# One-token attention and gated unit: every large load split by even and odd partitions over two DMA queues

## The chip, the cores and the metric

The kernel runs on one core of a Trainium2 chip. The core has a matrix engine (TensorE, PE in the profile), a vector engine (VectorE, DVE), a scalar engine (ScalarE, ACT), a general engine (GpSimd, POOL), an engine for synchronisation (SyncE, SP), and 16 DMA engines that move data between the chip's memory (DRAM in the names) and the core's own memory of 128 partitions. SyncE, ScalarE and GpSimd can issue transfers; each has its own queue. The metric is the time of one execution in microseconds (us), as the median of several. The profile's span, from the first to the last instruction, is a little shorter.

## The reference

Two branches work on one token `x` of 512 numbers, and a scalar gate mixes them. Everything is bfloat16.

```python
g = sigmoid((x * gate_w).sum())
# A: attention over the last W = 4096 positions of a cache of 65536
q = x @ wq                                  # 32 heads of 128; wq is 512 x 4096
s = q . k_cache[:, last 4096] * 128**-0.5   # 8 key heads, each used by 4 query heads
o = softmax(s) . v_cache[:, last 4096]
a = o @ wo                                  # wo is 4096 x 512
# B: gated unit
b = (sigmoid(x @ w_gate) * (x @ w_up)) @ w_down     # 512 -> 1792 -> 512
out = g * a + (1 - g) * b
```

With one token every weight and every cached key and value is used once. Read are 4 MB of wq, 8 MB of keys, 8 MB of values, 4 MB of wo and three matrices of 1.75 MB, 30.67 MB in the profile's count. The result is 512 numbers.

## The kernel before

All large loads are issued by SyncE, in the order in which they are needed, each as one transfer over all 128 partitions. `a` counts pairs of key heads; partition p = 2x + y of a tile of keys or values holds 64 consecutive positions of head 2a + y.

```python
nc.scalar.dma_start(xr[:, 0, :], A_x[0, :, :])               # x and gate_w: 1 KB each, by ScalarE
nc.scalar.dma_start(xr[:, 1, :], gate_w...)
dq = nc.sync
dq.dma_start(wq_sb[:], wq_v)                                 # 128 rows of 32 KB

def load_pair(t, cache, a, n0=0, n1=NP):
    dq.dma_start(t[:, n0:n1, :]..., cache[0, 2*a:2*a+2, SBASE:SBASE+W, :]...)    # 128 rows of 16 KB

kn = [...]                       # 4 tiles of keys, buffers "blk" (4 of them)
for a in range(HP): load_pair(kn[a], A_k_cache, a)
dq.dma_start(wg_sb[:], ...)      # w_gate
dq.dma_start(wu_sb[...], ...)    # w_up without its last part
for h in range(2):
    for b in range(2):           # the last part of w_up: 4 loads of 32 partitions
        dq.dma_start(wx_sb[32*b:32*b+32, h, :], wx_v[h, b])
vv = [...]                       # 4 tiles of values, in the buffers of the keys
for a in range(HP): load_pair(vv[a], A_v_cache, a)
for c0 in (0, 16): dq.dma_start(wo_sb[:, c0:c0+16, :], ...)          # wo in two halves
for j0, j1 in ((0,8), (8,11), (11,13), (13,14)):
    dq.dma_start(wd_sb[:, j0:j1, :], ...)                            # w_down in four parts

make_identity(nc, identf[:])     # GpSimd: identity and constants
...
for _ in range(4): nc.vector.memset(spare[:], 0.0)
...
```

After the front (x turned, the gate) the work follows the loads:

```python
# q = x @ wq, copied and transposed                       (needs wq)
# keys: VectorE transposes each tile (kT), TensorE multiplies into S_ps     (needs kn)
# gate branch, maximum, exponential, eT = transposed weights
for a in range(HP):
    for m in range(NP // 4):
        nc.tensor.matmul(pv_ps[32*a:32*a+32], lhsT=eT[:, a, 4*m:4*m+4, :], rhs=vv[a][:, 4*m:4*m+4, :], ...)
# up branch (glu), then o_ps -> oT -> oX -> oY: one column of oY for each 128 rows of wo
for c in range(NC_O): add_row(oY[:, c:c+1], wo_sb[:, c, :], ...)     # 32 x 2 matmuls
for j in range(NJ):   add_row(hT[:, j, 0:1], wd_sb[:, j, :], ...)    # 14 x 2 matmuls
nc.vector.tensor_copy(res[:, 0:HN], ...); nc.scalar.copy(res[:, HN:], ...)
nc.scalar.dma_start(out[0, :, :], res[:])
```

## Time and profile before

| | |
|---|---|
| time, median of 3 | 80.55 us (80.54 to 81.8) |
| span of the profiled execution | 78.7 us |
| TensorE busy | 52.5 us (67%) |
| VectorE busy | 38.8 us (49%) |
| ScalarE / GpSimd busy | 10.9 / 3.3 us |
| DMA | 30.71 MB in 2616 packets, mean 390 GB/s |
| tile of keys: issue to landing | 27.2 us (median of 4) |
| tile of values: issue to landing | 19.1 us (median of 4) |

How to read it: PE, DVE, ACT and POOL rows cut the span into 40 slices of about 2 us; each digit is the busy share in tenths. The DMA row is the mean busy share of the 16 DMA engines. "q1" is a DMA queue; its row gives packets, MB, and the time of its packets as a share of 16 engines' span. A line such as L290 is a line of the kernel. "out<-in" names the tile that an instruction writes and those that it reads. "<-DMA x" after an idle time says that a transfer into x ended the wait. The chain that ended last follows the last instruction back to what released it, step by step.

### The profile page before, as it was taken

To read this page: it belongs to the slowest core of one execution; us is meant where nothing else is said; L and a number is where in the kernel's file an instruction comes from. 1 tells how busy PE (TensorE), PEld (TensorE's weight loads), DVE (VectorE), ACT (ScalarE), POOL (GpSimd) and SP (SyncE) were. 2 spreads that over 40 slices of the span, in tenths; PEclk is the share of its full clock that TensorE was granted. 3 is DMA by queue.
4 is the path that set the end of the run, shared out by engine and by line. 5 is a ranking of instruction groups with operands and counts; after the bars stand their busy time and mean duration, and the time that the engine had idled before them with its cause. 6 is when DMAs were issued, how large, how long until landed. Compare 5 with 4: busy or idle time off the path is not lost.

```text
span 78.7 us, 798 instructions
## 1 busy us (share of the span) xinstructions
PE 52.5 (67%) x314; PEld 23.6 (30%) x314; DVE 38.8 (49%) x52; ACT 10.9 (14%) x20; POOL 3.3 (4%) x10
## 2 busy tenths in 40 slices
PE   0200094999905788898887307999996799567650
PEld 0200041344302333333332202344341345345420
DVE  1600920029869999999986349962000000690020
ACT  2400000247651000000002191000000002000010
POOL 7900000000000000000000000000000000000000
PEclk9999999999999999999999995699999999999997
DMA  7779799999999999999999999999999999999710
GB/s 184 300 316 533 316 483 391 408 425 458 441 408 416 425 474 416 386 437 417 438 410 426 441 416 441 408 433 441 416 433 433 424 425 433 416 391 409 290 42 1
DMA packets 2616, 30.71 MB, mean 390 GB/s; under 512 B 307, under 2 KB 438, under 8 KB 822
## 3 DMA queue, kind: packets, MB, share of 16 engines
q1 hardware_dynamic: 2608, 30.67, 92.9%
q8 instruction: 2, 0.03, 0.2%
q10 hardware_dynamic: 6, 0.00, 0.0%
HBM read 30.67 MB, written 0.00 MB: 390 GB/s over the span
## 4 chain that ended last, share of the span: by engine, by line
DMA 93%; SPq 2%; PE 1%; DVE 1%; issue 0%
DMA wd_sb<-in_B_w_down_dram 36%; DMA kn<-in_A_k_cache_dram 32%; DMA vv<-in_A_v_cache_dram 24%; SPq L84 2%; PE a_ps L290 1%; DVE res L341 1%; SPq L80 0%
## 5 line engine op out<-in xcount | busy, mean ns | idle before, releaser
L299 PE MATMUL pv_ps<-vv,eT 128*32 128x512 bf16 x64 | 15.9, 405 | 4.1 <-DVE eT L271 2.8
L227 PE MATMUL S_ps<-kT,qbig 128*128 128x512 bf16 x64 | 15.2, 378 | 5.0 <-DVE qbig L216 2.8
L188 DVE STREAM_TRANSPOSE kT<-kn 128x2048 f32<-128x2048 f32 x8 | 17.8, 2282 | 0.0
L227 PEld LDWEIGHTS <-qbig 128*128 128x128 bf16 x64 | 6.1, 97 | 14.1 <-issue 4.2
L299 PEld LDWEIGHTS <-eT 128*32 128x32 bf16 x64 | 6.2, 102 | 12.9 <-issue 4.2
L200 PE MATMUL q_ps<-wq_sb,xT 128*128 128x512 bf16 x32 | 8.8, 442 | 1.2 <-DMA wq_sb<-in_A_wq_dram 1.2
L318 DVE TENSOR_TENSOR oT<-o_ps,rb 128x32 bf16<-128x32 f32 x1 | 0.2, 191 | 13.5 <-PE o_ps L316 13.5
L205 DVE STREAM_TRANSPOSE qtT<-q_sb 128x512 f32<-128x512 f32 x4 | 2.7, 700 | 6.9 <-ACT q_sb L202 6.9
L182 PE MATMUL S_ps<-ident,other 2*128 2x512 bf16 x4 | 2.0, 611 | 5.8 <-DVE other L140 5.8
L202 ACT CAST q_sb<-q_ps 128x512 bf16<-128x512 f32 x8 | 4.7, 585 | 7.0 <-PE q_ps L200 7.0
L200 PEld LDWEIGHTS <-xT 128*128 128x128 bf16 x32 | 3.5, 111 | 6.8 <-issue 4.2
L290 PE MATMUL a_ps<-wo_sb,oY 128*1 128x256 bf16 x64 | 3.8, 272 | 1.5 <-DMA wo_sb<-in_A_wo_dram 1.2
L290 PEld LDWEIGHTS <-oY 128*1 128x1 bf16 x64 | 2.7, 83 | 3.1 <-issue 1.4
L271 DVE STREAM_TRANSPOSE eT<-e_sb 128x1024 bf16<-128x1024 bf16 x2 | 2.4, 1224 | 1.9 <-ACT e_sb L269 1.9
L254 ACT ACTIVATE sge<-gu_ps 128x448 f32<-128x448 f32 x1 | 0.5, 543 | 18.9 <-PE gu_ps L243 18.9
L309 ACT COPY pv_sb<-pv_ps 128x512 f32<-128x512 f32 x1 | 0.6, 585 | 17.7 <-PE pv_ps L299 17.7
L341 DVE CAST res<-a_ps 1x256 bf16<-1x256 f32 x1 | 0.4, 412 | 5.2 <-PE a_ps L290 5.2
L281 DVE RECIPROCAL sg<-sge 128x448 f32<-128x448 f32 x1 | 3.0, 2952 | 0.0
L165 DVE TENSOR_TENSOR gpr<-xr 1x512 f32<-1x512 bf16 x1 | 0.7, 679 | 4.6 <-DMA xr<-in_gate_w_dram 4.6
L249 DVE TENSOR_REDUCE pm<-S_ps 128x1 f32<-128x1024 f32 x2 | 2.4, 1208 | 0.9 <-PE S_ps L227 0.9
L290 PE MATMUL a_ps<-wd_sb,hT 128*1 128x256 bf16 x28 | 2.1, 271 | 0.8 <-DMA wd_sb<-in_B_w_down_dram 0.8
L148 PE MATMUL xt_ps<-ident,xr 1*128 1x1 bf16 x4 | 0.3, 165 | 3.5 <-POOL ident L126 3.5
(62 smaller groups left out, 31.0 us busy)
## 6 DMA issues: line engine op xcount, KB each, us to landing
kn<-in_A_k_cache_dram SPq DMA_DIRECT2D x4, 2048.0 KB, 27.2
vv<-in_A_v_cache_dram SPq DMA_DIRECT2D x4, 2048.0 KB, 19.1
wq_sb<-in_A_wq_dram SPq DMA_DIRECT2D x1, 4096.0 KB
wo_sb<-in_A_wo_dram SPq DMA_DIRECT2D x2, 2048.0 KB
wg_sb<-in_B_w_gate_dram SPq DMA_DIRECT2D x1, 1792.0 KB
wu_sb<-in_B_w_up_dram SPq DMA_DIRECT2D x1, 1456.0 KB
wd_sb<-in_B_w_down_dram SPq DMA_DIRECT2D x1, 1024.0 KB
wd_sb<-in_B_w_down_dram SPq DMA_DIRECT2D x1, 384.0 KB
```

What stands on the lines that cost most here:

```text
L84: dq.dma_start(t[:, n0:n1, :].rearrange("p n d -> p (n d)"), cache[0, 2 * a:2 * a + 2, SBASE:SBASE + W, :] .rearrange("y (x n) d -> x y n ...
L182: nc.tensor.matmul(S_ps[u // 2][:, u % 2, :], lhsT=other[:].rearrange("p o y u -> p (o y u)"), rhs=ident[0:2, 0:2].rearrange("p (o y) -> p ...
L188: nc.vector.transpose(t[:].bitcast(F32), kn[a][:, v * KB:(v + 1) * KB, :] .rearrange("p n d -> p (n d)").bitcast(F32))
L200: nc.tensor.matmul(q_ps[:], lhsT=xT[:, c:c + 1].to_broadcast([P, P]), rhs=wq_sb[:, c, ks], start=(c == 0), stop=(c == DC - 1))
L202: nc.scalar.copy(q_sb[:, ks], q_ps[:])
L205: nc.vector.transpose(qtT[:].bitcast(F32)[:, kq], q_sb[:].bitcast(F32)[:, kq])
L227: nc.tensor.matmul(S_ps[v][:, hb, :], lhsT=q_st[:, a, dhi, :, t], rhs=k_v[:, hb * 16:(hb + 1) * 16, dhi, :, t], start=False, stop=(a == HP ...
L249: nc.vector.tensor_reduce(pm2[:, v:v + 1], S_ps[v][:].rearrange("p a b -> p (a b)"), axis=AX.X, op=ALU.max)
L271: nc.vector.transpose(eT[:, :, v * KB:(v + 1) * KB, :].rearrange("p a n r -> p n a r"), e_sb[:, v, :].rearrange("p (n a r) -> p n a r", a= ...
L281: nc.vector.reciprocal(sg[:], sge[:])
L290: nc.tensor.matmul(a_ps[32 * i:32 * i + 1, i, 0:HN], lhsT=lhsT, rhs=rhs[:, i * HN:(i + 1) * HN], start=start, stop=stop)
L299: nc.tensor.matmul(pv_ps[32 * a:32 * a + 32, :, :], lhsT=eT[:, a, 4 * m:4 * m + 4, :].rearrange("p n r -> p (n r)"), rhs=vv[a][:, 4 * m:4 ...
```

## The change

Each large load becomes two: the even partitions are loaded from SyncE's queue, the odd ones from GpSimd's. For keys and values this means one head for each queue. It is for having two queues with work on the DMA engines at all times, in place of one. The order of the loads stays. The two small loads of x and gate_w move from ScalarE to GpSimd, ahead of GpSimd's part of wq; the other loads stand behind the set-up of constants, which GpSimd does in between. SyncE and GpSimd keep the order of the program. The four loads of the last part of w_up stay on SyncE alone. Four writes of VectorE to a spare cell go. A no-operation of SyncE behind the loads waits for the last 16 of them, so that these waits aren't left to the end of the program.

```diff
-    ORDERED = {mybir.EngineType.PE, mybir.EngineType.DVE, mybir.EngineType.Activation}
+    QUEUES = {mybir.EngineType.SP, mybir.EngineType.Pool}
+    ORDERED = QUEUES | {mybir.EngineType.PE, mybir.EngineType.DVE, mybir.EngineType.Activation}
 ...
+    ctx.enter_context(tc.manual_schedule(engines=QUEUES))
-    nc.scalar.dma_start(xr[:, 0, :], A_x[0, :, :])
-    nc.scalar.dma_start(xr[:, 1, :], gate_w.rearrange("(o n) -> o n", o=1))
+    nc.gpsimd.dma_start(xr[:, 0, :], A_x[0, :, :])
+    nc.gpsimd.dma_start(xr[:, 1, :], gate_w.rearrange("(o n) -> o n", o=1))
     dq = nc.sync
+    queues = (dq, nc.gpsimd)
+    loads = []
-    dq.dma_start(wq_sb[:], wq_v)
+    for y, queue in enumerate(queues):
+        queue.dma_start(wq_sb[y:P:2], wq_v[y:P:2])
 ... (here now stands the set-up: identity, ones, qbig, permT, other, selI)
-    spare = const.tile([1, 1], F32, name="spare")
-    for _ in range(4):
-        nc.vector.memset(spare[:], 0.0)
 ...
     def load_pair(t, cache, a, n0=0, n1=NP):
-        dq.dma_start(t[:, n0:n1, :].rearrange("p n d -> p (n d)"),
-                     cache[0, 2 * a:2 * a + 2, SBASE:SBASE + W, :]
-                     .rearrange("y (x n) d -> x y n d", n=NP)[:, :, n0:n1, :].rearrange("x y n d -> x y (n d)"))
+        for y, queue in enumerate(queues):
+            loads.append(queue.dma_start(t[y:P:2, n0:n1, :].rearrange("p n d -> p (n d)"),
+                                         cache[0, 2 * a + y, SBASE:SBASE + W, :].rearrange("(x n) d -> x n d", n=NP)
+                                         [:, n0:n1, :].rearrange("x n d -> x (n d)")))
 ... (w_gate, w_up, wo and w_down in the same manner; the four wx loads unchanged on dq)
+    seen = dq.nop()
+    for load in loads[-16:]:
+        tc.add_manual_dep(seen.ins, load.ins.name,
+                          mybir.DependencyInfo(mybir.DependencyClass.Sync, mybir.DependencyReason.DATA), reason="loads ended")
```

## The prediction

> **What bounds the kernel now.** I read the page first: the slices, the queues, the chain that ended last.

> ```profile
> span 78.7 us, 798 instructions
> ...
> PE   0200094999905788898887307999996799567650
> ...
> DVE  1600920029869999999986349962000000690020
> ...
> DMA  7779799999999999999999999999999999999710
> ...
> q1 hardware_dynamic: 2608, 30.67, 92.9%
> ...
> DMA 93%; SPq 2%; PE 1%; DVE 1%; issue 0%
> DMA wd_sb<-in_B_w_down_dram 36%; DMA kn<-in_A_k_cache_dram 32%; DMA vv<-in_A_v_cache_dram 24%; SPq L84 2%; PE a_ps L290 1%; DVE res L341 1%; SPq L80 0%
> ```

> The DMA row is at 9 almost to the end, one queue (SyncE's, q1) fills 92.9% of 16 engines' span, and the last chain is DMA for 93%. TensorE and VectorE have holes. So the question is how near the stream of 30.67 MB is to the best it can do. The windows of the steady part and of the end answer that (columns: stretch, its length, busy us and count of the five engines, granted clock, DMA share, GB/s):

> ```profile
> 20.00:30.00 10.00, 6.46 (x30) 2.60 (x28) 8.89 (x13) 2.51 (x5) 0.00 (x0) 1.00 1.00 428
> 50.00:60.00 10.00, 9.96 (x46) 4.14 (x44) 3.01 (x3) 0.00 (x0) 0.00 (x0) 0.97 1.01 429
> 60.00:70.00 10.00, 7.91 (x78) 4.25 (x76) 2.40 (x4) 0.58 (x1) 0.00 (x0) 1.00 0.99 420
> 70.00:72.00 2.00, 0.78 (x16) 0.51 (x13) 0.93 (x2) 0.00 (x0) 0.00 (x0) 1.00 0.96 392
> 72.00:74.00 2.00, 1.39 (x26) 0.98 (x24) 0.00 (x0) 0.00 (x0) 0.00 (x0) 1.00 0.93 367
> 74.00:75.50 1.50, 1.36 (x22) 0.86 (x19) 0.00 (x0) 0.00 (x0) 0.00 (x0) 1.00 0.51 184
> ```

> There is no hole in the steady part: share 1.00 at about 428 GB/s. Only the last 4 us sag. Last, the timeline of the end shows how much slack the arithmetic has (start, length, what, and in brackets the idle time before it with its releaser):

> ```profile
> 61.58 2.97 PE L299 MATMUL pv_ps<-vv,eT 128*32 128x512 bf16 x13 [1.28 <-DMA vv<-in_A_v_cache_dram]
> ...
> 68.24 1.91 PE L290 MATMUL a_ps<-wo_sb,oY 128*1 128x256 bf16 x32 [0.28 <-DVE oY L324]
> ...
> 71.38 1.91 PE L290 MATMUL a_ps<-wo_sb,oY 128*1 128x256 bf16 x32 [1.22 <-DMA wo_sb<-in_A_wo_dram]
> ...
> 73.90 1.46 PE L290 MATMUL a_ps<-wd_sb,hT 128*1 128x256 bf16 x22 [0.61 <-DMA wd_sb<-in_B_w_down_dram]
> ...
> 75.55 0.61 PE L290 MATMUL a_ps<-wd_sb,hT 128*1 128x256 bf16 x6 [0.19 <-DMA wd_sb<-in_B_w_down_dram]
> 76.20 0.41 DVE L341 CAST res<-a_ps 1x256 bf16<-1x256 f32 x1 [5.23 <-PE a_ps L290]
> ...
> 76.68 0.23 ACTq L343 DMA_DIRECT2D out_dram<-res  x1
> ```

> TensorE waits for the last value tile, for each part of wo and for wd. Its idle time before wo's second half, wd and wd's end is 1.22 + 0.61 + 0.19 = 2.0 us: so much later may the row oY come before the end moves, if no transfer moves. After the last landing (75.5) come 3.2 us of last matmuls, copy, store and end of program, which the change does not touch.

> [...]The trace agrees that sequencer time is no limit here: SyncE issues a load in 0.3 to 0.8 us, and a 2 MB load takes 4.9 us to move.[...] before, SyncE's issue at 0.73 has its first packet at 1.74, and GpSimd issues no load, so its figure is not shown.[...]

> **The change, part by part.**

> *The stream itself.* Bytes and rows stay the same: 64 rows of each tile go to each queue, each row as long as before (a kn row is 16 KB).[...] the trace has 1.74 to 75.38, 73.6 us.[...] the first rows of wq take about 2.0 us each instead of 1.21 (0.8); a 16 KB row takes 614 ns[...]; 304/16 = 19 completion marks of 9 ns (0.2); and the sag of the end (0.7). The sag: the 16 increments of one wd load arrive in two groups, 74.06 to 74.23 and 75.59 to 75.78. That gap appears after the wx loads and not before; these carry 344 KB, and if they use half of the engines, each of those has 43 KB more, 1.6 us at 27 GB/s. The change leaves wx as it is, on SyncE alone.[...] I put the expected saving at 0.4 us.

> *GpSimd starts late.* SyncE's half of wq is under way at 1.74 as before. GpSimd has to issue xr twice and then its half of wq;[...] its first big packet is at about 4.1. Until then SyncE's ring has all engines: no byte is lost, but SyncE is ahead by 2.4 us x 0.43 MB/us (428 GB/s), about 1.0 MB. With a fair turn from then on, a tile that needs both halves is complete up to 2.4 us later than before. wx gives some of it back: it is 344 KB of SyncE's alone, 0.8 us on the mean. So from vv on tiles come about 0.9 to 1.6 us later; I take 1.2.

> *What 1.2 us does at the end.* vv's last tile releases TensorE at 61.6 + 1.2 = 62.8; oY, 6.66 us behind it (68.24 - 61.58), at 69.4. wo's first half ends at 71.4; its second half lands at 71.4 + 1.2 = 72.6 and is done at 74.5. The first wd piece lands near 73.9 + 1.2 = 75.1; 28 matmuls x 66 ns (1.46/22) = 1.85 us, so 76.95 against 76.20 before: +0.7 us. A lag of 0.5 us would be absorbed; one of 2.4 us gives about +1.9.

> *The front.* xr moves from ScalarE to GpSimd, and the identity comes after three issues, perhaps 3 us later than its 3.4. VectorE's first chain waits for gate_w, which landed at 7.8 behind wq's rows; there is slack until wq at 12.98. Half of wq on GpSimd lands perhaps 1 us later. The query path then runs later, and TensorE's pv with it, by less than the 1.28 us that it waits for vv. Nothing at the end. The four spare writes that go cost VectorE 0.40 us in a stretch where it is idle: 0.

> *The nop and more semaphores.* At the end SyncE already waits for wd's loads one after the other (75.5 and 75.9) and then for the store. Twice as many loads mean up to eight more waits of some 28 ns (the duration of these waits in the trace); the nop takes them while the last matmuls run. 0, and +0.1 for extra waits of TensorE on both halves.

> Sum: -0.4 + 0.7 + 0.1 = +0.4 us on the mean, less something for the chance that the lag is small, so I set 80.6.

> **Rivals.**

> (1) *Two rings hide row overhead.*[...]

> (2) *The turn is not fair.* If SyncE's ring gets most of the bandwidth whenever both have work, GpSimd's halves of vv come only when SyncE is through. After its last vv half GpSimd still has its halves of wo and wd to move, 2 + 0.9 MB, at 0.43 MB/us 6.8 us before 75.4; so vv completes at 68.6, and 6.7 us to oY plus 3.8 for wo plus 1.9 for wd give 81.0, +4.8 us: 85. For it: gate_w, one small row on its own ring, waited from its issue at 1.28 to 7.8, behind about five rows of wq. Against: it did get in before wq was through.

> (3)[...] The steady rate would fall below 420 and each 1% costs 0.7 us. Against: the wx loads go to 32 partitions each, and the rate there stays above 400 GB/s.

> (4) *Nothing happens*[...]: within 0.3 us of before.

> **Range and chances.** (1) fully would be 79.0, (4) 80.5, the lag alone 81 to 82, (2) 85. I take 0.3 for some form of (1), 0.3 for (4), 0.25 for the lag as worked out, 0.15 for (2) or (3). 2% of 80.55 is 1.6 us:[...] slower than 82.2 needs a lag over 2 us or (2) or (3), 0.19; within, 0.64. Predicted 80.6 us, 8 times in 10 between 79.0 and 82.8.

> **What would show it.** A second big queue in the page with about 15.2 MB; the rate of 20 to 70 us at 428 (over 432 speaks for (1), under 422 for (3)); TensorE's release by the last vv at 62 to 64 instead of 61.6, and by wo's second half at 72 to 73; the last landing still at about 75.4. If the last landing comes over 0.8 us earlier, my view that the stream has nothing to give was wrong; if vv comes after 65, the turn is unfair; if the time from the last landing to the end changes by over 0.3 us, I misjudged the end of the program.

## The result, and the profile after

| | before | after |
|---|---|---|
| time, median of 4 | 80.55 us (80.44 to 81.8) | 83.88 us (83.86 to 85.43) |
| span of the profiled execution | 78.7 us | 82.1 us |
| last packet of the stream | 75.38 us | 75.56 us |
| last part of the last value tile lands | 61.5 us | 67.6 us |

The ratio is 1.0418, with an interval of 1.0394 to 1.0441: the change makes the kernel 4.2% slower, 3.3 us. It was predicted at 80.6 us, between 79.0 and 82.8. Of most kernels some executions are longer as a whole, by 1.2 to 3 us (81.8 and 85.43 us here); from here on, times are medians of the others.

The page of after, the lines that answer to those of before:

```profile
span 82.1 us, 832 instructions
...
PE   0000272099994199998888730079999989978970
...
DMA  1989999899999999999999999999999999993000
...
q1 hardware_dynamic: 1520, 15.51, 45.3%
q0 software_dynamic: 1312, 15.17, 43.5%
...
DMA 58%; PE 14%; DVE 13%; POOL 7%; issue 5%; DVEq 0%; POOLq 0%
```

The load is now on two queues (q1 is SyncE's, q0 GpSimd's), nearly equal in bytes. The DMA row is as full as before. What is new stands at the right end: in two slices TensorE stands at 9 and 7 while the DMA row is at 0. The chain of before was DMA for 93%; this one is DMA for 58%. Yet the stream ends as before, at 75.56: it has not become slower; arithmetic has moved behind its end. The windows of after say the same (columns as in the prediction, GB/s last):

```profile
20.00:30.00 10.00, 7.18 (x28) 2.81 (x27) 7.80 (x12) 4.77 (x9) 0.00 (x0) 0.88 1.00 427
50.00:60.00 10.00, 6.04 (x18) 2.28 (x18) 5.90 (x6) 1.42 (x4) 1.09 (x2) 0.66 1.02 433
60.00:70.00 10.00, 9.61 (x44) 4.02 (x44) 0.60 (x2) 0.00 (x0) 0.00 (x0) 1.00 0.99 420
...
72.00:74.00 2.00, 1.47 (x15) 0.99 (x9) 0.40 (x2) 0.00 (x0) 0.00 (x0) 1.00 0.94 367
74.00:75.50 1.50, 1.22 (x23) 0.94 (x24) 1.40 (x2) 0.00 (x0) 0.00 (x0) 1.00 0.50 191
```

427, 433 and 420 GB/s, against 428, 429 and 420 before, and the same sag at the end. But between 50 and 60 us TensorE works 6.04 us where it worked 9.96. The timeline of after shows what it waits for, first at the front, then at the end:

```profile
0.73 0.53 SPq L86 DMA_DIRECT2D wq_sb<-in_A_wq_dram  x1
1.25 0.64 POOL L76 DMA_DIRECT2D xr<-in_A_x_dram  x1 [0.81 <-POOLq L373]
...
2.37 0.56 POOL L86 DMA_DIRECT2D wq_sb<-in_A_wq_dram  x1
...
8.32 0.33 DVE L168 COPY xp<-xr 1x64 bf16<-1x64 bf16 x2 [8.32 <-DMA xr<-in_A_x_dram]
...
16.31 8.01 PE L215 MATMUL q_ps<-wq_sb,xT 128*128 128x512 bf16 x26 [3.39 <-DMA wq_sb<-in_A_wq_dram]
...
53.96 5.79 PE L314 MATMUL pv_ps<-vv,eT 128*32 128x512 bf16 x16 [5.08 <-DMA vv<-in_A_v_cache_dram]
...
67.67 2.98 PE L314 MATMUL pv_ps<-vv,eT 128*32 128x512 bf16 x13 [0.37 <-DMA vv<-in_A_v_cache_dram]
...
74.35 3.66 PE L305 MATMUL a_ps<-wo_sb,oY 128*1 128x256 bf16 x64 [0.28 <-DVE oY L339]
77.84 1.69 PE L305 MATMUL a_ps<-wd_sb,hT 128*1 128x256 bf16 x28
79.57 0.41 DVE L356 CAST res<-a_ps 1x256 bf16<-1x256 f32 x1 [2.49 <-PE a_ps L305]
...
80.06 0.50 ACTq L358 DMA_DIRECT2D out_dram<-res  x1
```

At the end: TensorE is released by the last value tile at 67.67 instead of 61.58, 6.1 us later. 6.68 us on comes oY (6.66 before). Then all 64 matmuls of wo and all 28 of wd run without one wait, 5.2 us, as everything has landed; before, 2.7 us more went by between oY and the copy res (76.20 - 68.24 = 7.96 against 79.57 - 74.35 = 5.22), in waits for wo and wd and in matmuls that ran between them. 6.1 - 2.7 = 3.4 us, the whole loss. As soon as the last values come late enough, the time is their landing plus a constant: 67.62 + 16.25 = 83.87.

At the front: GpSimd issues x at 1.25 and it lands at 8.3 (before, ScalarE's landed at 2.0), and wq is whole at 16.3 instead of 12.9.

Why the values come late is seen where the two halves of each tile are told apart. In the page's DMA issues of after (KB each, median us from issue to landing):

```profile
vv<-in_A_v_cache_dram SPq DMA_DIRECT2D x4, 1024.0 KB, 23.5
vv<-in_A_v_cache_dram POOLq DMA_DIRECT2D x4, 1024.0 KB, 19.6
```

SyncE's half of a value tile is under way for 4 us longer than GpSimd's, though SyncE was issued first and was ahead in the tiles of keys. A load's completion shows as 16 marks in the trace, one for each DMA engine (each is a packet of 4 bytes behind the load's rows, counted some 0.5 us after it: the last one of SyncE's vv 3 has its packet at 67.11 and its count at 67.62). The counts of after, in us, the first eight in order of time and the last eight, each from its first to its last:

```
                     first 8           last 8
vv 0, SyncE half     42.2 to 42.6      53.5 to 53.8
vv 0, GpSimd half    43.5 to 43.9      48.2 to 49.9
vv 3, SyncE half     56.8 to 58.5      67.2 to 67.6
vv 3, GpSimd half    54.7 to 55.1      62.9 to 64.6
```

The engines fall into two groups. The four wx loads (344 KB, the last part of w_up) have mark packets of eight engines only, and are complete at 40.5, 43.2, 46.0 and 48.9. Right behind them, the first value half of SyncE ends on eight engines at 42.4 and on eight at 53.6, 11.2 us later. On GpSimd's queue the gap is 4.7 us. TensorE is released (67.67) right behind the last mark of the last tile (67.62), so each tile waits for the slower queue on the slower engines.

### The profile page after: what moved, and what is told of

It is laid out like the page before. It is cut to its first block, busy times and chain, and to the rows that moved or that the text cites. A ratio compares the mean times of both kernels' runs of the same rounds, so it can differ in the third digit from the quotient of the medians.

```text
span 82.1 us, 832 instructions
## 1 busy us (share of the span) xinstructions
PE 54.1 (66%) x314; PEld 24.2 (29%) x314; DVE 37.7 (46%) x48; ACT 10.9 (13%) x20; POOL 13.5 (16%) x29
## 3 DMA queue, kind: packets, MB, share of 16 engines
q1 hardware_dynamic: 1520, 15.51, 45.3%
HBM read 30.67 MB, written 0.00 MB: 373 GB/s over the span
## 4 chain that ended last, share of the span: by engine, by line
DMA 58%; PE 14%; DVE 13%; POOL 7%; issue 5%; DVEq 0%; POOLq 0%
DMA kn<-in_A_k_cache_dram 29%; DMA vv<-in_A_v_cache_dram 29%; DVE kT L203 12%; PE a_ps L305 6%; PE pv_ps L314 4%; POOL qbig L97 2%; PE o_ps L331 1%; POOL kn L111 1%; POOL xr L76 1%; PE gu_ps L258 1%; POOL wq_sb L86 1%; PE gu_ps L255 1%; DVE res L356 0%; POOL permT L99 0%; POOL xr L77 0%
## 5 line engine op out<-in xcount | busy, mean ns | idle before, releaser
L314 PE MATMUL pv_ps<-vv,eT 128*32 128x512 bf16 x64 | 16.7, 420 | 5.5 <-DMA vv<-in_A_v_cache_dram 5.5
L242 PE MATMUL S_ps<-kT,qbig 128*128 128x512 bf16 x64 | 16.1, 401 | 4.1 <-DVE qbig L231 2.8
L215 PE MATMUL q_ps<-wq_sb,xT 128*128 128x512 bf16 x32 | 9.3, 462 | 3.4 <-DMA wq_sb<-in_A_wq_dram 3.4
L111 POOL DMA_DIRECT2D vv<-in_A_v_cache_dram x4 | 2.1, 536 | 33.3 <-DVE kT L203 33.3
L152 POOL DMA_DIRECT2D wd_sb<-in_B_w_down_dram x4 | 2.2, 544 | 7.6 <-DMA vv<-in_A_v_cache_dram 7.6
L324 ACT COPY pv_sb<-pv_ps 128x512 f32<-128x512 f32 x1 | 0.6, 585 | 19.9 <-PE pv_ps L314 19.9
```

Source lines behind the costliest of these rows:

```text
L111: loads.append(queue.dma_start(t[y:P:2, n0:n1, :].rearrange("p n d -> p (n d)"), cache[0, 2 * a + y, SBASE:SBASE + W, :].rearrange("(x n) ...
L152: loads.append(queue.dma_start(wd_sb[y:P:2, j0:j1, :], wd_v[y:P:2, j0:j1, :]))
L215: nc.tensor.matmul(q_ps[:], lhsT=xT[:, c:c + 1].to_broadcast([P, P]), rhs=wq_sb[:, c, ks], start=(c == 0), stop=(c == DC - 1))
L242: nc.tensor.matmul(S_ps[v][:, hb, :], lhsT=q_st[:, a, dhi, :, t], rhs=k_v[:, hb * 16:(hb + 1) * 16, dhi, :, t], start=False, stop=(a == HP ...
L314: nc.tensor.matmul(pv_ps[32 * a:32 * a + 32, :, :], lhsT=eT[:, a, 4 * m:4 * m + 4, :].rearrange("p n r -> p (n r)"), rhs=vv[a][:, 4 * m:4 ...
```

## The experiments

Four theories. *Turn by rows*: an engine with work on both queues takes a row of one, then a row of the other, however long each is. The wx loads have 32 rows of 2.7 KB each and use eight engines, four rows on each; so in these engines 16 short rows of SyncE are paired with 16 rows of 16 KB of GpSimd, and SyncE loses 16 rows there and none elsewhere. *Late front*: GpSimd starts late, x and wq are late, and this delay runs through. *Slow queue*: GpSimd's queue is slow as such. *Halves*: loads of every second partition are slow by themselves. In the expectations these are T, F, S and P, and a ring is a queue; in the first four (one queue, x on ScalarE, wx on both, wx over 16 engines) T still took a whole load, not a row, as what takes a turn. All edits but one start from the kernel after; each experiment computes the full result. All were timed against before, and the ratios compare the kernels best, as before itself moved by some 0.2 us between the rounds of runs.

### Halves on one queue

```diff
-    queues = (dq, nc.gpsimd)
+    queues = (dq, dq)
```

> All halves by parity stay, but both go to SyncE's queue; GpSimd loads only x and gate_w. T: one ring, no turns, the order of before: last value tile at 61.5, 80.6 us (80.2 to 81.2). S: also 80.6. F: wq complete at about 13 again, 80.6. P (the halves themselves are slow[...]): 83 to 84.

80.75 us, ratio 1.0033 (1.0018 to 1.0049). The timeline of this kernel:

```profile
61.85 2.98 PE L314 MATMUL pv_ps<-vv,eT 128*32 128x512 bf16 x13 [1.27 <-DMA vv<-in_A_v_cache_dram]
...
76.47 0.41 DVE L356 CAST res<-a_ps 1x256 bf16<-1x256 f32 x1 [5.22 <-PE a_ps L305]
```

The last values are back at 61.85. The split by parity, twice as many loads, x and gate_w on GpSimd (x lands at 8.3 here too) and the no-operation together cost 0.3%. The loss comes with the second queue for the large loads. *Halves* falls.

### x and gate_w back on ScalarE

```diff
-    nc.gpsimd.dma_start(xr[:, 0, :], A_x[0, :, :])
-    nc.gpsimd.dma_start(xr[:, 1, :], gate_w.rearrange("(o n) -> o n", o=1))
+    nc.scalar.dma_start(xr[:, 0, :], A_x[0, :, :])
+    nc.scalar.dma_start(xr[:, 1, :], gate_w.rearrange("(o n) -> o n", o=1))
```

> x and gate_w go back to ScalarE's queue, the four wx loads stay on SyncE. T: both rings start level, wq complete at 12.7 instead of 16.3, keys by 2 us earlier; but now SyncE falls behind by four places instead of three, the last value tile at 68.4 to 68.8: 84.6 us (84.0 to 85.4), slower than the changed kernel although its front is faster. F: the front is as before, so 80.5 (80.2 to 81.2). S and P: 83.9 less part of the front's gain, 82.5 to 83.9.

84.7 us (84.70 and 84.73), ratio 1.0519 (1.0494 to 1.0544), as expected. GpSimd now enters earlier, wq is whole at 14.5 instead of 16.3, SyncE issues its first value half at 29.3 instead of 30.8, and the kernel is slower still. The timeline of this kernel:

```profile
75.23 3.66 PE L305 MATMUL a_ps<-wo_sb,oY 128*1 128x256 bf16 x64 [0.28 <-DVE oY L339]
...
80.45 0.41 DVE L356 CAST res<-a_ps 1x256 bf16<-1x256 f32 x1 [2.50 <-PE a_ps L305]
```

SyncE's last value half lands at 68.5 (after: 67.6), GpSimd's at 62.8 (64.6). The late front was not the cause: it even helped, as it gave SyncE a lead on all engines, part of what SyncE then loses with wx. With a smaller lead it falls further behind. *Late front* falls as the cause of the loss.

### wx on both queues

```diff
-            dq.dma_start(wx_sb[32 * b:32 * b + 32, h, :], wx_v[h, b])
+            queues[b].dma_start(wx_sb[32 * b:32 * b + 32, h, :], wx_v[h, b])
```

> Theory T (turns): a DMA engine that has work on two rings serves one transfer of each ring in turn, whatever its size, so each of the four small wx loads on SyncE's ring costs that ring the place of one large load, and GpSimd's ring runs ahead by as many. With two wx loads on each ring the places are even again but for the one that GpSimd loses to xr: the last value tile complete at about 64 us instead of 67.6, TensorE's end near 76.9, time 81.2 us (80.6 to 81.8). Rival F (late front: GpSimd's half of wq comes 3.3 us late, so queries, key transposes and the issue of the value loads come late): nothing changes there, 83.9 +- 0.4. Rival S (GpSimd's software ring is slower or held up): 83.9 or slower, as it gets more loads. Rival P (halves by parity move more slowly): 83.9.

84.26 us, ratio 1.0464 (1.0444 to 1.0485): a miss. In the DMA issues of this kernel the two queues have changed places:

```profile
vv<-in_A_v_cache_dram SPq DMA_DIRECT2D x4, 1024.0 KB, 15.6
vv<-in_A_v_cache_dram POOLq DMA_DIRECT2D x4, 1024.0 KB, 23.4
```

Two loads for each queue do not take the same turns on each engine. A wx load of SyncE leaves 9 marks, one about 1.2 us after its issue, without a packet (in after at 6.43 for the load issued at 5.24), and one from each of eight engines; the same load from GpSimd leaves 16 marks, eight at 41.4 to 41.7 and eight at 45.3 to 47.3. The packets tell what it does: GpSimd's two loads leave 32 packets of 5,376 bytes, each two rows of wx, 32 of 8 bytes, and 32 marks, where SyncE's leave 64 rows and 16 marks. By their times a load of GpSimd has two of the large packets on each of eight engines and two of 8 bytes on each of the other eight. So GpSimd loses turns also on the eight engines on which SyncE loses none, on top of the lead that SyncE has there, and its last value half lands at 68.05 (SyncE's: 60.7). 68.05 + 16.25 = 84.3, the measured time. I had counted loads for each queue and not packets for each engine. The 16 marks of GpSimd's load, with its rows on eight engines, don't tell by themselves where the rows lie.

### wx in one load over 16 engines

```diff
-    wx_v = B_w_up.rearrange("(h b j i c) f -> h b i j c f", h=2, b=2, j=4, i=8)[:, :, :, :, DC - 1, F - FX:F]
-    for h in range(2):
-        for b in range(2):
-            dq.dma_start(wx_sb[32 * b:32 * b + 32, h, :], wx_v[h, b])
+    wx_v = B_w_up.rearrange("(h p c) f -> h p c f", h=2, c=DC)[:, :, DC - 1, F - FX:F]
+    dq.dma_start(wx_sb[:], wx_v.rearrange("h p f -> p h f"))
... (the copy of x that goes with it takes the same order)
```

> wx as one transfer of 64 rows in their natural order, still on SyncE. T: SyncE loses one place where it lost four, which evens the one that GpSimd lost to xr: last value tile at 61.3 to 62; and if the 344 KB now spread over all 16 engines, all engines end together, some 0.8 us earlier. Time 79.9 us (79.3 to 80.6). F: 83.9, less at most 0.8 for the even end: 83.1. S and P: the same 83.1 to 83.9. If a turn is four rows and not one transfer, this load of eight rows an engine counts as two places, and the value tile comes at about 64: 80.8.

82.80 us, ratio 1.0279 (1.025 to 1.0308): 1.1 us better than after, but a miss by 2 to 3. The two groups of engines are gone: the last value half lands at 63.5 on 15 engines, and at 65.06 on one. Eight short rows on every engine cost SyncE eight places: from ahead it goes to some two rows behind (vv 0: GpSimd 47.9, SyncE 50.4; 2.5 us are two rows of each queue). What was not foreseen is the rate. The windows of this kernel (GB/s last):

```profile
30.00:38.00 8.00, 7.70 (x32) 3.19 (x31) 8.00 (x5) 0.00 (x0) 1.08 (x2) 0.89 1.00 425
38.00:44.00 6.00, 5.40 (x24) 2.20 (x23) 6.00 (x3) 0.00 (x0) 0.54 (x1) 1.00 1.03 340
46.00:60.00 14.00, 9.85 (x52) 4.04 (x51) 8.40 (x12) 3.02 (x6) 2.53 (x5) 0.88 1.00 427
```

While wx passes, all engines are busy (1.03) but move 340 GB/s instead of 425: 6 us x 0.2 = 1.2 us of stream lost, and the stream ends that much later (76.5 on most engines). GpSimd's rows of wu beside wx took 592 ns at the median (572 to 749) instead of 441. Why they took longer, no run shows.

### All rows level: x, gate_w and wx on ScalarE

```diff
-    nc.gpsimd.dma_start(xr[:, 0, :], A_x[0, :, :])
-    nc.gpsimd.dma_start(xr[:, 1, :], gate_w.rearrange("(o n) -> o n", o=1))
+    nc.scalar.dma_start(xr[:, 0, :], A_x[0, :, :])
+    nc.scalar.dma_start(xr[:, 1, :], gate_w.rearrange("(o n) -> o n", o=1))
...
-            dq.dma_start(wx_sb[32 * b:32 * b + 32, h, :], wx_v[h, b])
+            nc.scalar.dma_start(wx_sb[32 * b:32 * b + 32, h, :], wx_v[h, b])
```

> x, gate_w and the four wx loads all go to ScalarE's queue; SyncE and GpSimd keep only the halves of equal rows. Turns theory: neither of the two rings loses a place to a small load, so both halves of each tile land within about 2.5 us of each other; last value tile at 61.5 to 62.3, 80.6 us (80.2 to 81.3). If GpSimd's ring as such is the trouble, the value tiles stay late and it is 82.5 or more.

80.85 us, ratio 1.0057 (1.0041 to 1.0073). With the same rows on both large queues, the second queue costs 0.6%, not 4.2%: *slow queue* falls too. The timeline of this kernel:

```profile
63.03 2.97 PE L314 MATMUL pv_ps<-vv,eT 128*32 128x512 bf16 x13 [1.29 <-DMA vv<-in_A_v_cache_dram]
...
76.61 0.41 DVE L356 CAST res<-a_ps 1x256 bf16<-1x256 f32 x1 [4.20 <-PE a_ps L305]
```

The last values are 1.4 us later than before and the end only 0.4 us: so late, the end still hangs on landings, as the 64 matmuls of wo take 5.33 us from oY on, where they take 3.66 in after, which has no wait there. The wx loads, now on a third queue, show the turn directly. They land at 14.7, 20.0, 25.3 and 30.6, 5.3 us apart for 84 KB each. An engine has four of a load's rows; if between two of them it serves one 16 KB row of each large queue, that is 4 x (0.61 + 0.61) + 0.43 = 5.3 us, where 0.61 us is a row of 16 KB and 0.43 four short rows of 0.11 (both as in after).

### The same rows of wx in eight loads

```diff
-    for h in range(2):
-        for b in range(2):
-            dq.dma_start(wx_sb[32 * b:32 * b + 32, h, :], wx_v[h, b])
+    for b in range(2):
+        for j in range(4):
+            dq.dma_start(wx_sb[32 * b + j:32 * b + 32:4, :, :], wx_v[:, b, :, j].rearrange("h i f -> i h f"))
```

> The same wx bytes and rows on SyncE, in eight transfers with two rows on each of eight engines, where there were four with four rows. If a turn is a whole transfer, SyncE falls back by eight places on these engines: last value tile near 69.1, 85.3 us. If an engine alternates between the rings row by row (the size of a row does not count), the rows are as many as before and only the marks at the end of each transfer are more: last value tile at 67.5 to 68.5, 84.2 us (83.8 to 84.8).

Is it rows that take a place, or whole loads? 86.22 us, ratio 1.0721 (1.0698 to 1.0745): a miss, and nearer the 85.3 for whole loads than the 84.2 for rows. The landings say otherwise. The eight wx loads land between 39.4 and 52.3, mostly 1.4 to 2 us apart, where the four of after were 2.8 us apart: half the rows in a load, about half the time. On seven of the eight engines with wx rows SyncE's last value half ends at 68.1 to 68.5, as expected for rows; on the eighth it ends at 69.99, and 69.99 + 16.25 = 86.24, the measured time. That engine fell behind by 1.5 us at once, between 42.4 and 45.6, when a fetch of instructions ran (at 42.6; see the last section). In after the first fetch (at 44.8) fell among the other eight engines: in SyncE's half of vv 1 seven of them mark from 46.96 to 47.33 and one at 48.67.

The packets show the turn itself. The trace gives start, end, size and queue of each packet, not its engine; but nearly every packet (2,776 of 2,837 in after) starts 3 to 4 ns before the end of another, so they can be chained, and 16 chains come out, taken here as the 16 engines (in some stretches one breaks off and goes on as a seventeenth). Parts of one chain each (S, G and A: a row of SyncE's, GpSimd's or ScalarE's queue, 16 KB long; with x: a row of wx; with h: of 8 KB; with a point: a mark):

```
after                    Sx G  Sx G  Sx G  Sx G  S. G  Sx G. Sx G  Sx G
wx in eight loads        Sx G  Sx G  S. G  Sx G. Sx G  S. G  Sx G  Sx G
all rows level           Ax G S  A. G. S  Ax G S  Ax G S.  Ax G S  Ax G S
half as long rows        S Gh  S Gh  S. Gh  S Gh  S G.  S Gh  S Gh
```

### w_up whole, without wx

```diff
-    dq.dma_start(wu_sb[:].rearrange("p c f -> p (c f)")[:, 0:LM], ...[:, 0:LM])
-    ... (the four wx loads and the matmuls that used them)
+    dq.dma_start(wu_sb[:], B_w_up.rearrange("(p c) f -> p c f", c=DC))
```

> The kernel before, with w_up loaded whole in one transfer of 128 rows of 14 KB, so that no wx load falls on half of the engines (four matmuls less, the two little ones and the copies for x in wx order go too). All engines end together, 0.7 to 0.8 us earlier: 79.8 us (79.5 to 80.3). If the two groups of landings have another cause, 80.5.

This one starts from *before*: 81.2 us, ratio 1.0105 (1.0085 to 1.0125): a miss, as I thought the sag of the end was wx's doing and could be had back. The windows of the end of this kernel:

```profile
74.00:75.50 1.50, 1.11 (x20) 0.85 (x21) 0.00 (x0) 0.00 (x0) 0.00 (x0) 1.00 0.24 88
75.50:77.00 1.50, 0.91 (x12) 0.35 (x8) 0.38 (x1) 0.34 (x1) 0.00 (x0) 1.00 0.02 8
```

Fourteen engines have their last mark between 74.5 and 75.1, a sag earlier than before's: 0.24 of the engines are busy where it was 0.51. But two go on to 76.1 and 76.3. In between, two blocks of 16 KB of instructions were moved, 1.07 and 1.1 us long (the page's row "q8 instruction: 2, 0.03"), at 39.3 and 70.0; one engine's marks are late from the first on and a second's from the second on, so these two are taken to have moved them. In before, with fetches at 39.6 and 69.45, nine engines mark late behind the wx rows (the first value load: 46.5 to 46.8, the other seven 45.1 to 45.3), and ten after the second fetch (the last load: 75.5 to 75.8, the other six 74.1 to 74.3): the eight with wx rows and those with a fetch. So there the fetches fall on engines that have no wx rows, and hide behind those that do. Taking wx away bares them.

The same without wx, with two queues: the kernel after, w_up whole in halves, x and gate_w on ScalarE.

```diff
-        queue.dma_start(wu_sb[:].rearrange("p c f -> p (c f)")[y:P:2, 0:LM], ...[y:P:2, 0:LM])
-    ... (the four wx loads and what used them)
+        queue.dma_start(wu_sb[y:P:2], wu_v[y:P:2])
...
-    nc.gpsimd.dma_start(xr[:, 0, :], ...)        (and gate_w)
+    nc.scalar.dma_start(xr[:, 0, :], ...)        (and gate_w)
```

> The changed kernel with w_up whole, in two halves, and with x and gate_w on ScalarE: two rings with equal rows and nothing else. Turns theory: both halves together, the last value tile near 61.5, no uneven end: 79.9 us (79.5 to 80.4), level with one ring and whole w_up. If two level rings hide row overhead: 78.5 to 79.2. If two rings cost something even when level: 80.5 or more.

81.44 us, ratio 1.0125 (1.0106 to 1.0144), against 81.2 on one queue. This pair is the cleanest test of what two queues are for: same bytes, same rows, no odd loads, one queue or two (the halves double the number of loads, and the no-operation is there). Two are not faster: the stream takes 74.0 us on one queue (1.77 to 75.81) and 74.2 on two (2.05 to 76.24), so no saving is seen.

### Half as long rows on one queue

To the level kernel above:

```diff
-        load_pair(vv[a], A_v_cache, a)
+        for y, queue in enumerate(queues):
+            for n0, n1 in ((0, NP),) if y == 0 else ((0, NP // 2), (NP // 2, NP)):
+                loads.append(queue.dma_start(vv[a][y:P:2, n0:n1, :]..., A_v_cache[0, 2 * a + y, ...][:, n0:n1, :]...))
```

> The kernel with level rings (x, gate_w and wx on ScalarE), but GpSimd loads its half of each value tile in two transfers whose rows are 8 KB in place of 16; the bytes are the same. If an engine takes rows in turn from the rings whatever their size, GpSimd gets a third of the bytes during the value loads; by rows, its last value half ends about 26.5 us after the first begins at 43, near 69.5 to 70.5, and the time is 86.2 us (85.0 to 87.5). If the turn goes by bytes, nothing changes: 80.9 (80.6 to 81.5).

Here GpSimd's value halves go in rows of 8 KB and SyncE's in rows of 16 KB. If the turn goes by bytes, nothing changes; if by rows, GpSimd gets one byte for SyncE's two. 83.32 us, ratio 1.0337 (1.0315 to 1.0359), between the two expectations. Between 45 and 60 us, in steps of 3 us, the packets of GpSimd move 127 to 162 GB/s and those of SyncE 264 to 300: one to two. The page of this kernel, then its timeline:

```profile
vv<-in_A_v_cache_dram POOLq DMA_DIRECT2D x8, 512.0 KB, 24.3
```

```profile
67.14 2.97 PE L318 MATMUL pv_ps<-vv,eT 128*32 128x512 bf16 x13 [0.25 <-DMA vv<-in_A_v_cache_dram]
...
79.02 0.41 DVE L360 CAST res<-a_ps 1x256 bf16<-1x256 f32 x1 [2.49 <-PE a_ps L309]
```

The turn does not go by bytes. (Whole loads in turn would also give one to two here, as GpSimd's are half as large; the chains above rule them out.) My size for it was too large, as TensorE starts on the last tile when the first of GpSimd's two loads for it is there (67.1; the second lands at 68.7), and 67.1 + 16.25 = 83.35.

### Only wx to ScalarE

```diff
-            dq.dma_start(wx_sb[32 * b:32 * b + 32, h, :], wx_v[h, b])
+            nc.scalar.dma_start(wx_sb[32 * b:32 * b + 32, h, :], wx_v[h, b])
```

> The changed kernel with only the four wx loads moved to ScalarE's queue; x and gate_w stay on GpSimd, so GpSimd's half of wq still comes late. Rows in turn: SyncE stays about four rows ahead and no more; last value tile at 62.8 to 63.8, 81.3 us (80.7 to 81.9). If the late front matters more than the wx rows: 83 or more.

81.2 us, ratio 1.0069 (1.0043 to 1.0094): 344 KB of 30.67 MB on another queue, and 3.5 of the 4.2% are gone. The timeline of this kernel:

```profile
51.95 6.51 PE L314 MATMUL pv_ps<-vv,eT 128*32 128x512 bf16 x16 [2.78 <-DVE eT L286]
...
65.12 2.97 PE L314 MATMUL pv_ps<-vv,eT 128*32 128x512 bf16 x13 [0.15 <-DMA vv<-in_A_v_cache_dram]
```

The wait for the first values, 5.08 us in after, has become the 2.78 us for the weights eT that before has too. SyncE's last half lands at 59.0 and GpSimd's at 65.1, later than I had put it: SyncE now keeps the lead that GpSimd's late start gives it. Against the level kernel the values are 2.1 us later; in time the two are not told apart (1.0069 and 1.0057, with intervals that overlap).

### Without the no-operation

```diff
-    seen = dq.nop()
-    for load in loads[-16:]:
-        tc.add_manual_dep(seen.ins, load.ins.name, ...)
```

> The changed kernel without SyncE's no-operation; the waits for the loads then stand at the end of the program. They can pass while the last matmuls run, as the loads are long in: 83.9 us (83.6 to 84.2). If they pass only behind the wait for the store, eight waits of about 60 ns come on top: 84.4.

84.07 us, ratio 1.043 (1.0406 to 1.0454), and after has 1.0418 (1.0394 to 1.0441): the no-operation makes no difference that can be seen.

By the ratios the loss adds up so: everything of the change but the second queue, 0.3%; two level queues in place of one, 0.6% in all; x and gate_w on GpSimd with them, 0.7%, a step too small to be told from none; wx on SyncE, 4.2%. So 3.5 of the 4.2% are the wx rows. No version ran faster than before.

## Why the prediction was wrong

*The stream itself: right.* It ends at 75.56, predicted "at about 75.4"; 427 to 433 GB/s, predicted 428. The "expected saving" of 0.4 us was an estimate that no trace showed; it is 0, as the pair 81.44 and 81.2 shows.

*GpSimd starts late: the mechanism right, the size wrong.* I had GpSimd's "first big packet" at "about 4.1", an estimate that rested on no trace; it is at 8.7. GpSimd took 0.5 to 0.64 us for an issue, but issuing wasn't what it waited for. The first packet of x came at 6.26, when each engine had served three rows of wq from SyncE, and x landed behind the fourth; GpSimd's wq came after that and two rows of keys. By then SyncE had moved four rows of 32 KB and two of 16 KB on each engine: the lead was some 2.6 MB, not 1.0. The hint stood in the profile of before: gate_w, issued at 1.28, landed at 7.8. I quoted it for the second rival and did not use it here. Without the wx rows this lead alone put the last values at 65.1, not 62.8.

*The step that failed: "wx gives some of it back: it is 344 KB of SyncE's alone, 0.8 us on the mean".* I took "a fair turn" as fair in bytes, and the mean over 16 engines. The turn is fair in packets, so in rows, and these rows are on eight engines. There, 16 rows of 2.7 KB go against 16 rows of 16 KB: 16 x (0.61 + 0.1) = 11.4 us by the durations, 11.2 by the marks. On these engines SyncE goes from some five rows ahead to some eleven behind (its first value half, at 53.6, ends just before GpSimd's fourth, at 54.8); on the others it stays ahead. Every tile needs both. In place of a last value tile at 62.8 the runs have 67.6 with wx on SyncE and 65.1 without. The 0.8 us on the mean should have been a loss of 11 us on half of the engines.

*What it does at the end: right as arithmetic.* With the measured landing in it, 67.62 + 6.66 + 3.8 + 1.85 = 79.9; measured 79.57. The rule that a lag up to 2.0 us costs little held in the level kernel (1.4 us late, 0.4 us at the end). The 1.9 us for a lag of 2.4 was too much: with only wx moved, a lag of 3.5 us cost 0.7%, some 0.6 us.

*The front: half right.* wq was 3.3 us later, not 1, and keys and queries with it; that this does nothing at the end was right, as the run with an early front (84.7 us) and the one with halves on a single queue show.

*The no-operation: right*, 0. The spare writes were not tested alone; they lie within the 0.3% of the kernel with one queue.

*The sag: half right.* wx does use half of the engines (9 marks), and it does make the two groups. The ten late marks of the last load, at 75.52 to 75.84, are eight engines with wx rows and two that fetched instructions. So the 0.7 us aren't there to be had: without wx the engines with the fetches end last (81.2 us).

*The rivals.* The second was nearest in numbers (values at 68.6, 85 us) and its sign, "if vv comes after 65, the turn is unfair", came true. Its reason was not: SyncE isn't served first when both have work; it is SyncE that falls behind, so that the number came near is luck. The third, that halves by odd and even partitions move more slowly, falls by the kernel with one queue (80.75 us) and in its sign, a rate under 422 GB/s in the steady part (427 and 433 measured from 20 to 30 and from 50 to 60 us); something like it was seen only when wx went over 16 engines (340 GB/s). The first falls by the pair (its 79.0 was an estimate for a saving that no trace showed), and the fourth by the 4.2%.

My range could not hold it: 0.15 for the second and third rivals together was too little for something that I had not tried to follow engine by engine.

## What to carry to other kernels

Before splitting loads over two queues, list the rows (and the marks) that each queue gives to each DMA engine, not the bytes: as far as these runs show, an engine takes one packet, so one row, from each queue in turn, so a few short rows on one queue hold back all that stands behind them, at the price of the other queue's long rows (here 16 rows of 2.7 KB held back SyncE's values by 11.2 us on eight engines). A tile that is split over two queues is complete when the slower of them is (67.6 us here, where the faster was through at 64.6), so give both the same rows, and put odd small loads on a queue on which nothing urgent waits behind them (here ScalarE's: 81.2 us where SyncE's gave 83.88). Where one queue already kept all the engines busy, at 428 GB/s, a second gained nothing (81.44 us with two, 81.2 with one).

## What the runs showed of the hardware that was not expected

- A queue that came later waited for several long rows before the turns began: in after, x, issued at 1.25 us, had its first packet at 6.26, after three rows of 32 KB of wq on each engine, and landed at 8.3, behind the fourth. It was 2.0 where ScalarE issued it together with wq.
- The completion mark of a load, 4 bytes and 9 ns, takes a turn as a row of 16 KB and 612 ns does (the chains of after).
- A load of 32 rows of 2.7 KB ran on eight engines from SyncE's queue, four rows and a mark on each (9 marks in all). From GpSimd's queue, in the kernel with wx on both, the rows went in packets of two (5,376 bytes), two packets on each of eight engines, and the other eight got two packets of 8 bytes and a mark (16 marks).
- One load of 128 rows of 2.7 KB into 64 partitions over 16 engines brought the stream from 425 to 340 GB/s while it lasted, and the rows of 11.6 KB beside it from 441 ns to 592 at the median.
- Two fetches of instructions, 16 KB and 1.0 to 1.1 us each, ran on the same DMA engines. In the kernel with w_up whole, on one queue, such an engine ended over 1 us after the others (marks at 76.1 and 76.3 against 74.5 to 75.1).
